# Value products turned round, a sum of exponentials by TensorE, and one accumulator in the last step

## The chip, the cores and the metric

The kernel runs on one core of one Trainium2 chip. The metric is the device time of one execution in microseconds (us). Before the change it is 943.63 us, the median of 3 runs (942.25 to 943.75).

## The reference

```python
def _attn_ref(q, k, v, agents):            # q, k, v: 2 x 12480 x 128, agents: 2 x 49 x 128
    def sm(a, b):
        s = scale * (a @ b.transpose(0, 2, 1))
        s = s - s.max(-1, keepdims=True)
        e = np.exp(s)
        return e / (e.sum(-1, keepdims=True) + 1e-09)
    a2k = sm(agents, k)                    # 49 x 12480 per batch
    agent_v = a2k @ v                      # 49 x 128 per batch
    q2a = sm(q, agents)                    # 12480 x 49 per batch
    return q2a @ agent_v

def _moe_ref(x, w_in, w_out):              # x: 24960 x 128, w_in: 128 x 2048, w_out: 2048 x 128
    h = x @ w_in
    g = np.where(h > 0.0, h, np.exp(np.minimum(h, 0.0)) - 1.0)
    return g @ w_out
```

The weights come as 64-bit floats and are turned into 32-bit ones on the chip. All is computed in 32 bits; the two large products use a high and a low part of each operand.

## The kernel before

Of each batch the 12480 rows are cut into 13 groups of 960, and a group into 8 tiles (R) of 120 rows (TP). The kernel has a prologue, in which batch 0's side of the agents is done and the weights are converted, and then a loop of 416 steps (S) and 4 more (LAG). A step is one half group (480 columns) times 256 of the 2048 hidden columns, so 8 steps (NP) make a half and 16 a group, here called a turn.

What a step does: `p1(s)` multiplies the attention of the half with `w_in` times the agents' values (line 443, six matmuls of 480 columns, with 49 or 50 rows in each half of the array); `elu(s)` takes the exponential on ScalarE (line 449) and the rest of the activation on VectorE (line 451); `split(s)` makes the high part on ScalarE (line 213) and the low part (line 218) on GpSimd in two halves, or, in steps that `is_kept` names, on VectorE in one instruction; `p2(s - 4)` adds the product with `w_out` of four steps earlier (line 479, 12 matmuls of 480 columns, upper and lower 64 rows into the two accumulators `o0` and `o1`). After each half the accumulators are read by VectorE (`ob`, line 491) and ScalarE (`oa`, line 494), added by GpSimd and stored. `is_kept` names two to three of each eight steps; in such a step the activation stays in PSUM, where its tile `h` is held until the low part is made. There are three tiles `h`, used also by the visits below.

The agents' side of batch 1 is spread over the loop in visits: `plan` puts each in a step, and `visit` gets a tile `h` and does two jobs in it. Up to step 75 a visit holds scores of keys (`k`, line 174) and queries (`q`, line 305): 32 matmuls of 49 columns into four strips of 32 rows. In steps 83 to 155 it holds value products (`e`, `ev_pe`, line 233): the exponentials `s_all` of one group, 64 columns of them, are the stationary operand and 129 columns of `v` the moving one (128 values and a column of ones, whose product is the sum of the exponentials). Eight matmuls alternate between the upper and the lower 64 rows of the output. `ev1_out` adds the outcome on VectorE to `sv` (line 248). There are four pairs (`e e`) and five visits of a query job and a value job (`q e`). After the last one `av_pe` (lines 252 and 253) turns `sv` round by a matmul with `dup`, which holds identities, and `av_out` takes the agents' values `av["t"]` and the reciprocal sum `av["rz"]` from PSUM.

In the prologue the same product is done for batch 0 (jobs `v0` to `v12`, accumulated in PSUM), and `o0 o1 o2` are its `ev0_out`, `av_pe` and `av_out`; jobs `f` are matmuls on a tile `warm` whose result nobody uses. The order of the jobs in the prologue is that of the words in the `run(...)` strings, in the loop that of the calls in it (lines 790 to 815), and engines take their instructions in that order. The first `p1` needs `A0` (line 271), which needs `av["t"]` and `av["rz"]`.

In the last step, ScalarE reads `o0` in two halves (line 487), VectorE adds `o1` (line 488), and SyncE issues the two stores.

Of the kernel before, what the change touches and what calls it, by code (L numbers as in the profile page):

```python
# [24 lines left out]
def tile_agent_attention_moe(  # L25
# [201 lines left out]
    ev_ps, av = {}, {}  # L227

    def ev_pe(ps, b, r, rs):
        e = s_all[:, r].rearrange("p t a -> p (t a)")  # L230
        for j in range(R):
            u = ROWS[j % 2]
            nc.tensor.matmul(out=ps[u:u + 64], lhsT=e[:, j * NA:j * NA + 64], rhs=v_t[b, r][:, j, :], start=(r == rs[0] and j < 2), stop=(r == rs[-1] and j >= R - 2))  # L233
        v_t.pop((b, r))

    def ev0_pe(r):
        ev_pe(ev_ps[0], 0, r, range(NR))

    def ev0_out():
        av["sv"] = sm_p.tile([128, VW], F32, tag="sv", name="sv")  # L240
        nc.vector.tensor_copy(out=av["sv"], in_=ev_ps.pop(0))

    def ev1_out(ps, r):
        if r == 0:
            av["sv"] = sm_p.tile([128, VW], F32, tag="sv", name="sv")
            nc.vector.tensor_copy(out=av["sv"], in_=ps)
        else:
            nc.vector.tensor_tensor(out=av["sv"], in0=av["sv"], in1=ps, op=ALU.add)

    def av_pe():  # L250
        ps = attn_bank()
        nc.tensor.matmul(out=ps[:C, 0:NA2], lhsT=av["sv"][:, 0:C], rhs=dup, start=True, stop=True)
        nc.tensor.matmul(out=ps[:NA2, 128:129], lhsT=dup, rhs=av["sv"][:, C:C + 1], start=True, stop=True)
        av["ps"] = ps

    def av_out():
        ps = av.pop("ps")
        attn_free(ps)
        av["t"] = sm_p.tile([C, NA2], F32, tag="avt", name="avt")
        nc.vector.tensor_copy(out=av["t"], in_=ps[:C, 0:NA2])  # L260
        rz = sm_p.tile([NA2, 1], F32, tag="rz", name="rz")
        nc.vector.tensor_scalar(out=rz, in0=ps[:NA2, 128:129], scalar1=1e-9, scalar2=None, op0=ALU.add)
        nc.vector.reciprocal(out=rz, in_=rz)
        av["rz"] = rz

    def A_pe(b, lo, hi, ps=None):
        av[b, lo] = attn_bank() if ps is None else ps
# [156 lines left out]
    def is_kept(s):  # L424
        first = s - s % NP
        steps = visits.values()
        if first + EDGE in steps:
            kind = "late"
        elif first + 1 in steps:
            kind = "early"  # L430
        else:
            kind = "turn" if first // NP % 2 == 0 else None
        return s - first in ((3,7) if s < NP else KEPT[kind])

    def p1(s):
# [31 lines left out]
    def p2(s):  # L467
        j, half, c = at_step(s)
        if c == 0:
            o_t[0] = ps_o.tile([128, 512], F32, tag="o0", name="o0")  # L470
            o_t[1] = ps_o.tile([128, 512], F32, tag="o1", name="o1")
        first, last = c == 0, c == NP - 1
        hi, lo = hi_t.pop(s), lo_t.pop(s)
        jobs = [(w[:, c, i], hi[:, i, :]) for w in (w_lo, w_hi) for i in range(2)]
        jobs += [(w_hi[:, c, i], lo[:, i, :]) for i in range(2)]
        for i, (w, v) in enumerate(jobs):
            for u, r in enumerate(ROWS):
                x = slice(r, r + 64)
                nc.tensor.matmul(out=o_t[u][:, 0:T], lhsT=w[x], rhs=v[x, :], start=first and i == 0, stop=last and i == len(jobs) - 1)  # L479
        if last:  # L480
            oa = o_p.tile([128, T], F32, tag="oa", name="oa")
            ob = o_p.tile([128, T], F32, tag="ob", name="ob")
            pa, pb = o_t[0], o_t[1]
            n = j * G + half * T
            if s == S - 1:
                for x in (slice(0, T // 2), slice(T // 2, T)):
                    nc.scalar.activation(out=oa[:, x], in_=pa[:, x], func=ACTF.Identity, bias=ncs[:, 0:1])
                    nc.vector.tensor_tensor(out=ob[:, x], in0=pb[:, x], in1=oa[:, x], op=ALU.add)
                    nc.sync.dma_start(out=outT[:, n + x.start:n + x.stop], in_=ob[:, x])
                return None  # L490
            nc.vector.tensor_copy(out=ob, in_=pb[:, 0:T])  # L491
# [20 lines left out]
    with tc.manual_schedule():  # L512
        with tc.tile_pool(name="pro", bufs=6) as pro, tc.tile_pool(name="wc", bufs=2) as wc_p:
# [35 lines left out]
            ev_ps[0] = two[:, 0, 0:VW]  # L549

            def busy(n, cols=512):
                for _ in range(n):
# [56 lines left out]
            def w_diag():  # L609
# [17 lines left out]
                "v": ev0_pe,  # L627
# [3 lines left out]
                "o": lambda n: (ev0_out, av_pe, av_out, w_acc, w_diag)[n](),  # L631
# [26 lines left out]
            run("s12 r12 c12 M1 f5")  # L658
            run("M2 M3 f3 M4 M5 Q0 f2")
            run("u0 x0 U2 u1 x1 U4 Q1 Q2 Q3 x2 u3 x3 U6 u5 x4 x5 u7 Q4 Q5 U8 x6 x7 u9 x8 Q6 U10 u11 x9 U12 x10 x11 x12 a5 b5 a6 b6")  # L660
            run("v0 +o3,v9,v10,v11,v12,q1,K0,K1 v1 v2 v3 v4 Q7 f2 v5 Q8 d5 g5 h5 l5 d6 g6 v6 f1 v7 f1 v8 W0 f2 a7 Q9 b7 h6 l6 d7 g7 h7 l7 v9 f2 v10 v11 v12 W1")
            run("o0 o1 W2 o2")
            fill_ps = ps_o.tile([128, 512], F32, tag="o0", name="o0")
            a_banks.update({0: fill_ps, 1: pair[:, 0, :], 2: hk[:, 0, :], 3: fill_ps})
            run("A0 A1 A2 z0 z1 z2")
# [184 lines left out]
```

## Time and profile before

| | before |
|---|---|
| median of 3 runs | 943.63 us |
| profiled execution, its own time | 942.42 us |
| its span, first to last instruction | 940.6 us |
| TensorE, PE (share of the span) | 929.9 us, 99% |
| ScalarE, ACT | 853.1 us, 91% |
| VectorE, DVE | 758.7 us, 81% |
| GpSimd, POOL | 800.7 us, 85% |
| mean granted TensorE clock | 0.999 |

A busy share is an average over the stages, and matmuls are pipelined, so that 99% is not TensorE at its peak. What a change is worth is read from the chain of waits, the work that ended last followed back from the end. A 32-bit matmul stands in the trace as two records, so 32 matmuls of the program are x64 there; products of high and low parts are one record each.

### The profile page before, as it was taken

The page shows a single profiled execution, that of the slowest core. Times are in us where ns is not written, and L with a number is a line of the kernel's source. Part 1 is how long each engine was busy: PE and PEld are TensorE (multiplying, and loading weights), DVE is VectorE, ACT ScalarE, POOL GpSimd, SP SyncE. Part 2 cuts the span into 40 slices and gives each one's busy share as a digit, 9 for nine tenths or more (in the row PEclk, how much of TensorE's full clock was granted, in tenths as well). Part 3 has the DMA queues.
Part 4 walks back from the last instruction along what each step waited for, and adds up shares of the span by engine and source line. Part 5 has one row for each costly group of instructions (what it writes and reads, how often), then busy time and mean ns, then how long its engine had stood idle before and what let it go on. Part 6 is the DMA issues. An engine that isn't in the chain of part 4 may idle for free.

```text
span 940.6 us, 26784 instructions
## 1 busy us (share of the span) xinstructions
PE 929.9 (99%) x11136; PEld 813.8 (87%) x11136; DVE 758.7 (81%) x861; ACT 853.1 (91%) x1024; POOL 800.7 (85%) x686
## 2 busy tenths in 40 slices
PE   8999999999999999999999999999999999999998
PEld 6878889888888888989888888888888888899997
DVE  6877877878878778878878888887888888888876
ACT  4679999999899889999999999999999999999996
POOL 2578898898899899899898898889898898988886
PEclk9999999999999999999999999999999999999999
DMA  9942222242232211012101101011020021001000
GB/s 351 407 160 70 82 97 70 84 116 70 77 100 71 70 43 49 29 44 71 38 22 61 39 28 65 28 46 59 16 81 28 22 71 38 28 13 39 28 22 22
DMA packets 26108, 67.11 MB, mean 71 GB/s; under 512 B 3221, under 2 KB 14955, under 8 KB 25987
## 3 DMA queue, kind: packets, MB, share of 16 engines
q1 hardware_dynamic: 25843, 65.36, 21.1%
q8 instruction: 87, 1.43, 0.6%
q14 instruction: 34, 0.28, 0.1%
q10 hardware_dynamic: 144, 0.05, 0.0%
HBM read 43.11 MB, written 12.78 MB: 59 GB/s over the span
## 4 chain that ended last, share of the span: by engine, by line
PE 95%; DMA 2%; POOL 1%; ACT 1%; issue 0%; DVE 0%; SPq 0%; DVEq 0%; ACTq 0%
PE o L479 57%; PE h L443 29%; PE h L233 3%; PE h L305 2%; PE h L174 1%; DMA raw<-in_w_out_dram 1%; POOL lo L218 1%; DMA k<-in_kT_dram 1%; PE h L553 1%; PE h L343 1%; DMA py<-px 0%; PE h L271 0%; PE o L174 0%; PE o L505 0%; ACT hi L213 0%
## 5 line engine op out<-in xcount | busy, mean ns | idle before, releaser
L218 POOL TENSOR_TENSOR lo<-g,hi 128x480 fp32r<-128x480 f32 x576 | 692.1, 1236 | 45.7 <-ACT hi L213 26.3
L449 ACT ACTIVATE e<-h 128x960 f32<-128x960 f32 x416 | 406.3, 977 | 39.6 <-PE h L443 23.7
L451 DVE SCALAR_TENSOR_TENSOR g<-e,h 128x960 f32<-128x960 f32 x288 | 331.8, 1152 | 117.1 <-ACT e L449 80.3
L213 ACT ACTIVATE hi<-g 128x960 fp32r<-128x960 f32 x288 | 289.4, 1005 | 1.2 <-DVE g L451 1.2
L479 PE MATMUL o<-lo,w_hi 64*128 64x480 f32 x1664 | 258.0, 379 | 0.5 <-POOL lo L218 0.2
L479 PE MATMUL o<-hi,w_lo 64*128 64x480 f32 x1664 | 257.3, 379 | 0.1
L479 PE MATMUL o<-hi,w_hi 64*128 64x480 f32 x1664 | 256.5, 378 | 0.0
L443 PE MATMUL h<-py,ahi 50*128 50x480 f32 x832 | 253.4, 384 | 0.4 <-DMA py<-px 0.4
L443 PE MATMUL h<-px,ahi 50*128 50x480 f32 x832 | 253.2, 384 | 0.1
L479 PEld LDWEIGHTS o<-lo,w_hi 64*128 64x128 f32 x1664 | 165.6, 184 | 22.9 <-POOL lo L218 2.5
L479 PEld LDWEIGHTS o<-hi,w_hi 64*128 64x128 f32 x1664 | 165.4, 184 | 18.4
L479 PEld LDWEIGHTS o<-hi,w_lo 64*128 64x128 f32 x1664 | 164.5, 186 | 18.6 <-issue 0.3
L443 PEld LDWEIGHTS h<-px,ahi 50*128 50x128 f32 x832 | 151.9, 186 | 13.7 <-DVE ob L491 1.1
L443 PEld LDWEIGHTS h<-py,ahi 50*128 50x128 f32 x832 | 152.0, 186 | 11.3 <-issue 0.9
L451 DVE SCALAR_TENSOR_TENSOR h<-e,h 128x960 f32<-128x960 f32 x128 | 148.0, 1156 | 15.0 <-ACT e L449 13.9
L218 DVE TENSOR_TENSOR lo<-h,hi 128x960 fp32r<-128x960 f32 x128 | 147.5, 1152 | 12.7 <-ACT hi L213 12.7
L443 PE MATMUL h<-px,alo 49*128 49x480 f32 x416 | 156.6, 377 | 0.0
L443 PE MATMUL h<-py,alo 49*128 49x480 f32 x416 | 156.5, 376 | 0.0
L213 ACT ACTIVATE hi<-h 128x960 fp32r<-128x960 f32 x128 | 124.6, 974 | 0.0
L495 POOL TENSOR_TENSOR ob<-ob,oa 128x480 f32<-128x480 f32 x51 | 63.2, 1239 | 58.6 <-ACT oa L494 25.5
L443 PEld LDWEIGHTS h<-px,alo 49*128 49x128 f32 x416 | 78.0, 188 | 5.6
L443 PEld LDWEIGHTS h<-py,alo 49*128 49x128 f32 x416 | 78.1, 188 | 4.3
(111 smaller groups left out, 529.3 us busy)
## 6 DMA issues: line engine op xcount, KB each, us to landing
k<-in_kT_dram SPq DMA_DIRECT2D x26, 480.0 KB
q<-in_qT_dram SPq DMA_DIRECT2D x26, 480.0 KB
out_dram<-ob SPq DMA_DIRECT2D x51, 240.0 KB
v<-in_vx_dram SPq DMA_DIRECT2D x13, 483.8 KB
v<-in_vx_dram SPq DMA_DIRECT2D x12, 516.0 KB
py<-px SPq DMA_DIRECT2D x50, 93.8 KB
py<-px SPq DMA_DIRECT2D x50, 91.9 KB
raw<-in_w_in_dram SPq DMA_DIRECT2D x4, 512.0 KB
```

The costliest lines, as they stand in the source:

```text
L174: nc.tensor.matmul(out=ps[u:u + w, j * NA:(j + 1) * NA], lhsT=src[:, x:x + w], rhs=ag_sb[:, b, :], start=True, stop=True)
L213: nc.scalar.activation(out=out, in_=x, func=ACTF.Copy)
L218: eng.tensor_tensor(out=out, in0=x, in1=hi.bitcast(F32), op=ALU.subtract)
L233: nc.tensor.matmul(out=ps[u:u + 64], lhsT=e[:, j * NA:j * NA + 64], rhs=v_t[b, r][:, j, :], start=(r == rs[0] and j < 2), stop=(r == rs[-1 ...
L305: nc.tensor.matmul(out=ps[u:u + w, t * NA:(t + 1) * NA], lhsT=src[:, x:x + w], rhs=ag_sb[:, j // NG, :], start=True, stop=True)
L343: nc.tensor.transpose(ps[:NA2, u, i * HP:(i + 1) * HP], pp[x, i, 0:NA2], ident[x, x])
L443: nc.tensor.matmul(out=h[:, u, 0:T], lhsT=a[x, :], rhs=p[u ^ half][x, :], start=i == 0, stop=i == 2)
L449: nc.scalar.activation(out=e, in_=h, func=ACTF.Exp, bias=-1.0, scale=1.0)
L451: nc.vector.scalar_tensor_tensor(out=g, in0=e, scalar=1.0, in1=h, op0=ALU.min, op1=ALU.max)
L479: nc.tensor.matmul(out=o_t[u][:, 0:T], lhsT=w[x], rhs=v[x, :], start=first and i == 0, stop=last and i == len(jobs) - 1)
L495: nc.gpsimd.tensor_tensor(out=ob, in0=ob, in1=oa, op=ALU.add)
L553: nc.tensor.matmul(out=two[:, 1, 0:cols], lhsT=warm[:, 0:128], rhs=warm[:, 0:cols], start=True, stop=True)
```

## The change

1. `ev_pe` becomes `evt_pe`: `v` is now the stationary operand, in four strips of 32 of its columns, and 49 exponentials the moving one. A group takes 32 matmuls of 49 columns instead of 8 of 129, and the outcome is the agents' values already turned round. `av_pe` and `av_out` go.
2. The sum of the exponentials no longer comes with the product. In batch 0 TensorE sums them with a stationary tile of ones (`Z0` to `Z12`, 4 matmuls of 98 columns each), VectorE folds that (`Y0`) and one matmul adds the partitions (`Y1`). In batch 1 VectorE sums each group's exponentials (`z_red`, from SBUF) and folds them in `z_dup`; one matmul in the visit `A` at step 163 adds the partitions, and `z_out` takes the reciprocal there.
3. In steps 80 to 159 the second half of a turn keeps steps 1, 5 and 7 in PSUM; before, 1 and 7. Subtractions (`e_sub`) and exponentials (`e_exp`) of batch 1 move by one step in places.
4. In the last step all 128 rows go at once into `o1` (6 matmuls instead of 12); `o0` ends a step earlier and is read by ScalarE meanwhile, and the second half of the last store is issued by ScalarE.

```diff
-    def ev_pe(ps, b, r, rs):
-        e = s_all[:, r].rearrange("p t a -> p (t a)")
+    def evt_pe(ps, b, r, rs):
         for j in range(R):
-            u = ROWS[j % 2]
-            nc.tensor.matmul(out=ps[u:u + 64], lhsT=e[:, j * NA:j * NA + 64], rhs=v_t[b, r][:, j, :], start=(r == rs[0] and j < 2), stop=(r == rs[-1] and j >= R - 2))
+            for u in range(0, C, 32):
+                nc.tensor.matmul(out=ps[u:u + 32, 0:NA], lhsT=v_t[b, r][:, j, u:u + 32], rhs=s_all[:, r, j, :], start=r == rs[0] and j == 0, stop=r == rs[-1] and j == R - 1)
...
+    def z_red(r):
+        nc.vector.tensor_reduce(out=m_all[:, :, r], in_=s_all[:, r, 0:R, :].rearrange("p t a -> p a t"), axis=AX.X, op=ALU.add)
+
+    def z_dup():
+        nc.vector.tensor_reduce(out=dup[:TP, 0:NA], in_=m_all, axis=AX.X, op=ALU.add)
+        nc.vector.tensor_copy(out=dup[:TP, ROWS[1]:ROWS[1] + NA], in_=dup[:TP, 0:NA])
...
+        if 80 <= s < 160 and first // NP % 2 == 1:
+            return s - first in (1,5,7)
...
+            if s == S - 1:
+                nc.tensor.matmul(out=o_t[1][:, 0:T], lhsT=w, rhs=v, start=False, stop=i == len(jobs) - 1)
+                continue
...
+        if s == S - 2:
+            o_t[2] = o_p.tile([128, T], F32, tag="oa", name="oa")
+            return lambda: nc.scalar.activation(out=o_t[2], in_=o_t[0][:, 0:T], func=ACTF.Identity, bias=ncs[:, 0:1])
...
-                for x in (slice(0, T // 2), slice(T // 2, T)):
-                    nc.scalar.activation(out=oa[:, x], in_=pa[:, x], func=ACTF.Identity, bias=ncs[:, 0:1])
-                    nc.vector.tensor_tensor(out=ob[:, x], in0=pb[:, x], in1=oa[:, x], op=ALU.add)
-                    nc.sync.dma_start(out=outT[:, n + x.start:n + x.stop], in_=ob[:, x])
+                for x, eng in ((slice(0, T // 2), nc.sync), (slice(T // 2, T), nc.scalar)):
+                    nc.vector.tensor_tensor(out=ob[:, x], in0=pb[:, x], in1=o_t[2][:, x], op=ALU.add)
+                    eng.dma_start(out=outT[:, n + x.start:n + x.stop], in_=ob[:, x])
...
+            def z0_pe(r):
+                if r == 0:
+                    zt.append(ps_o.tile([128, 512], F32, tag="o0", name="o0"))
+                for i in range(4):
+                    nc.tensor.matmul(out=zt[0][32 * i:32 * i + 32, 0:2 * NA], lhsT=ones2[:, 0:32], rhs=s_all[:, r, 2 * i:2 * i + 2, :].rearrange("p t a -> p (t a)"), start=r == 0, stop=r == NR - 1)
...
-            run("v0 +o3,v9,v10,v11,v12,q1,K0,K1 v1 v2 v3 v4 Q7 f2 v5 Q8 d5 g5 h5 l5 d6 g6 v6 f1 v7 f1 v8 W0 f2 a7 Q9 b7 h6 l6 d7 g7 h7 l7 v9 f2 v10 v11 v12 W1")
-            run("o0 o1 W2 o2")
+            run("v0 +o3,v9,v10,v11,v12,q1,K0,K1 Z0 v1 Z1 v2 Z2 v3 Z3 v4 Z4 Z5 Q7 f2 v5 Q8 d5 g5 h5 l5 d6 g6 Z6 v6 Z7 f1 v7 Z8 f1 v8 W0 Z9 Z10 f1 a7 Q9 b7 h6 l6 d7 g7 h7 l7 v9 Z11 Z12 f2 Y0 v10 f1 v11 v12 Y1")
+            run("W1 o0 W2")
...
+            at(-1 + s0 if r == NR - 1 else s0 + (4, 3, -1)[r % 3], z_red, r)
         s0 = visits["e", NR - 1]
-        at(s0 + 2, av_pe)
-        at(s0 + 2, av_out)
+        at(s0 + 2, z_dup)
+        at(s0 + 1, avt_dup)
...
+            if lo == 0:
+                nc.tensor.matmul(out=tile[:NA2, 0, 256:257], lhsT=dup[:TP, :], rhs=onec[:TP, :], start=True, stop=True)
             for i in range(2):
                 A_pe(1, lo + 512 * i, lo + 512 * i + 512, tile[:, i, :])
+            if lo == 0:
+                z_out(tile[:NA2, 0, 256:257])
```

Three places in the order. First TensorE in the prologue, from job `v5` to the end of `v12`; before:

```order
L233 MATMUL h<-v,s_all 64x129 x16
L553 MATMUL h<-warm 128x128
L233 MATMUL h<-v,s_all 64x129 x8
L553 MATMUL h<-warm 128x128
L233 MATMUL h<-v,s_all 64x129 x8
L505 MATMUL o_708<-w_hi,allone 128x512
L505 MATMUL o_708<-w_lo,allone 128x512
L553 MATMUL h<-warm 128x128 x2
L233 MATMUL h<-v,s_all 64x129 x8
L553 MATMUL h<-warm 128x128 x2
L233 MATMUL h<-v,s_all 64x129 x24
```

The same place after, from the end of `v7`'s part on (line 235 is `evt_pe`, line 605 `z0_pe`, line 555 the matmuls nobody uses):

```order
L555 MATMUL h<-warm 128x128
L235 MATMUL h<-s_all,v 32x49 x32
L508 MATMUL o_963<-w_hi,allone 128x512
L508 MATMUL o_963<-w_lo,allone 128x512
L605 MATMUL o_624<-s_all,ones_83 32x98 x8
L555 MATMUL h<-warm 128x128
L235 MATMUL h<-s_all,v 32x49 x32
L605 MATMUL o_624<-s_all,ones_83 32x98 x8
L555 MATMUL h<-warm 128x128 x2
L235 MATMUL h<-s_all,v 32x49 x32
L555 MATMUL h<-warm 128x128
L235 MATMUL h<-s_all,v 32x49 x64
```

The products of the groups now stand in more and shorter runs with the sums between them, and the unused matmuls are as many, but in more places.

Second VectorE at a visit with a query job and a value job (step 107, tiles `mx` and `qe` are the query's, `lo` the low part of a kept step); before:

```order
L491 COPY ob<-o_4600 128x480
L222 TENSOR_TENSOR s_all<-s_all,mb 120x392
L451 SCALAR_TENSOR_TENSOR g<-e,h 128x960
L310 TENSOR_REDUCE mx<-h 124x8
L318 TENSOR_TENSOR qe_87<-h,mx 124x8x49
L248 TENSOR_TENSOR sv<-sv,h 128x129
L451 SCALAR_TENSOR_TENSOR g<-e,h 128x960 x2
L326 TENSOR_REDUCE z<-qe_87 124x8
L222 TENSOR_TENSOR s_all<-s_all,mb 120x392
L451 SCALAR_TENSOR_TENSOR g<-e,h 128x960
L330 RECIPROCAL qz<-z 124x8
```

After:

```order
L247 TENSOR_REDUCE m_all<-s_all 120x49
L494 COPY ob<-o_5090 128x480
L225 TENSOR_TENSOR s_all<-s_all,mb 120x392
L449 SCALAR_TENSOR_TENSOR g<-e,h 128x960
L306 TENSOR_REDUCE mx<-h 124x8
L314 TENSOR_TENSOR qe_90<-h,mx 124x8x49
L244 TENSOR_TENSOR avt<-avt,h 128x49
L449 SCALAR_TENSOR_TENSOR g<-e,h 128x960
L225 TENSOR_TENSOR s_all<-s_all,mb 120x392
L449 SCALAR_TENSOR_TENSOR h<-e,h 128x2x480
L322 TENSOR_REDUCE z<-qe_90 124x8
L449 SCALAR_TENSOR_TENSOR g<-e,h 128x960
```

A sum (line 247) is new ahead of the copy `ob`, the second subtraction stands a step earlier, and one more activation goes to `h`, whose low part follows on VectorE.

Third TensorE at the end of the program; before, the last four of the 12 matmuls:

```order
L479 MATMUL o_14721<-lo,w_hi 128x480
L479 MATMUL o_14722<-lo,w_hi 128x480
L479 MATMUL o_14721<-lo,w_hi 128x480
L479 MATMUL o_14722<-lo,w_hi 128x480
L846 UNCONDITIONAL_BRANCH
```

After, all six of the last step:

```order
L476 MATMUL o_15405<-hi,w_lo 128x480 x2
L476 MATMUL o_15405<-hi,w_hi 128x480 x2
L476 MATMUL o_15405<-lo,w_hi 128x480 x2
L878 UNCONDITIONAL_BRANCH
```

The last step writes one accumulator alone.

## Rows read from the trace of the kernel before

**Rows 1.** The page: shares of the chain that ended last, and the granted clock.
```profile
PEclk9999999999999999999999999999999999999999
PE 95%; DMA 2%; POOL 1%; ACT 1%; issue 0%; DVE 0%; SPq 0%; DVEq 0%; ACTq 0%
```

**Rows 2.** Chain of waits, visits with scores alone: start us, us, what.
```profile
113.56 0.83 PE h L305 x64
114.39 0.69 PE h L174 x64
...
131.05 1.52 PE h L174 x96
```

**Rows 3.** Chain of waits, a visit `e e` and the value part of a `q e`.
```profile
236.87 1.92 PE h L233 x32
...
255.89 1.03 PE h L233 x16
```

**Rows 4.** Chain of waits, the turning round of batch 1's values.
```profile
402.89 0.41 PE h L252 x2
403.30 0.11 PE h L253 x2
```

**Rows 5.** Chain of waits in the prologue.
```profile
34.08 4.56 PE h L233 x80
...
39.63 0.64 PE h L553 x4
40.27 1.91 PE h L233 x32
42.19 0.42 PE h L553 x2
42.61 1.03 PE h L233 x16
...
47.87 2.80 PE h L233 x48
...
51.33 0.21 PE h L252 x2
51.54 0.10 PE h L253 x2
```

**Rows 6.** Chain of waits at the end.
```profile
933.90 2.66 PE o L479 x24
936.57 0.46 ACT oa L487
...
937.05 0.76 DVE ob L488 x2
```

**Rows 7.** Timeline at the end, SyncE's queue: start us, us, instruction.
```profile
937.49 0.81 SPq L489 DMA_DIRECT2D out_dram<-ob  x2
```

**Rows 8.** Groups by form: names, shapes, count | busy us, mean ns | idle before.
```profile
L218 POOL TENSOR_TENSOR lo<-g,hi 128x480 fp32r<-128x480 f32 x576 | 692.1, 1236 | 45.7 <-ACT hi L213 26.3 <-POOL ob L495 10.5 <-POOL lo L218 7.5
L218 DVE TENSOR_TENSOR lo<-h,hi 128x960 fp32r<-128x960 f32 x128 | 147.5, 1152 | 12.7 <-ACT hi L213 12.7
L326 DVE TENSOR_REDUCE z<-qe 124x8 f32<-124x400 f32 x26 | 14.6, 563 | 0.0
L248 DVE TENSOR_TENSOR sv<-sv,h 128x129 f32<-128x129 f32 x12 | 3.4, 283 | 0.1
```

**Rows 9.** Busy time by stretch: us, PE, PEld, DVE, ACT, POOL busy, clock, DMA.
```profile
201.60:236.90 35.30, 35.30 (x493) 29.98 (x494) 29.64 (x37) 33.10 (x40) 31.80 (x27) 1.00 0.30 82
236.90:272.90 36.00, 36.00 (x410) 30.60 (x412) 28.39 (x34) 32.33 (x39) 32.39 (x28) 1.00 0.30 81
254.00:266.00 12.00, 12.00 (x174) 10.07 (x172) 10.62 (x15) 10.22 (x13) 10.52 (x9) 1.00 0.38 104
```

**Rows 10.** Timeline at the visit `A` of step 163, VectorE and ScalarE.
```profile
416.06 1.15 DVE L451 SCALAR_TENSOR_TENSOR g<-e,h 128x960 f32<-128x960 f32 x1
...
416.91 1.02 ACT L281 ACTIVATE ahi<-h,unit,rz 114x256 fp32r<-114x256 f32 x2
```

More of the change, by code (lines that the diff above doesn't have):

```diff
@@ L70, in tile_agent_attention_moe @@
     ones = const.tile([NA, TP], F32)
+    ones2 = const.tile([TP, 32], F32)
+    part = const.tile([128, 1], F32)
+    onec = const.tile([128, 1], F32)
     pp = const.tile([TQ, R // 2, 128], F32)
@@ L225, in e_exp @@
         nc.scalar.activation(out=s_all[:, r, 0:R, :], in_=s_all[:, r, 0:R, :], func=ACTF.Exp, scale=scale)
-    ev_ps, av = {}, {}
-    def ev_pe(ps, b, r, rs):
-        e = s_all[:, r].rearrange("p t a -> p (t a)")
+    av = {}
+    def evt_pe(ps, b, r, rs):
         for j in range(R):
-            u = ROWS[j % 2]
-            nc.tensor.matmul(out=ps[u:u + 64], lhsT=e[:, j * NA:j * NA + 64], rhs=v_t[b, r][:, j, :], start=(r == rs[0] and j < 2), stop=(r == rs[-1] and j >= R - 2))
+            for u in range(0, C, 32):
+                nc.tensor.matmul(out=ps[u:u + 32, 0:NA], lhsT=v_t[b, r][:, j, u:u + 32], rhs=s_all[:, r, j, :], start=r == rs[0] and j == 0, stop=r == rs[-1] and j == R - 1)
@@ L234, in ev_pe @@
         v_t.pop((b, r))
[L236 to L241, printed above, removed]
     def ev1_out(ps, r):
         if r == 0:
-            av["sv"] = sm_p.tile([128, VW], F32, tag="sv", name="sv")
-            nc.vector.tensor_copy(out=av["sv"], in_=ps)
-        else:
-            nc.vector.tensor_tensor(out=av["sv"], in0=av["sv"], in1=ps, op=ALU.add)
@@ L250, in av_pe @@
[L250 to L260, printed above, removed]
+            av["t"] = sm_p.tile([C, NA2], F32, tag="avt", name="avt")
@@ new lines, in ev1_out @@
+            nc.vector.memset(av["t"][:, NA:], 0.0)
+            nc.vector.tensor_copy(out=av["t"][:, 0:NA], in_=ps)
+        else:
+            nc.vector.tensor_tensor(out=av["t"][:, 0:NA], in0=av["t"][:, 0:NA], in1=ps, op=ALU.add)
+    def z_red(r):
[3 more added lines that the diff above has]
+        nc.vector.tensor_copy(out=dup[:TP, ROWS[1]:ROWS[1] + NA], in_=dup[:TP, 0:NA])
@@ L261, in av_out, with z_out, avt_dup @@
+    def z_out(x):
         rz = sm_p.tile([NA2, 1], F32, tag="rz", name="rz")
-        nc.vector.tensor_scalar(out=rz, in0=ps[:NA2, 128:129], scalar1=1e-9, scalar2=None, op0=ALU.add)
+        nc.vector.tensor_scalar(out=rz, in0=x, scalar1=1e-9, scalar2=None, op0=ALU.add)
         nc.vector.reciprocal(out=rz, in_=rz)
         av["rz"] = rz
+    def avt_dup():
+        nc.vector.tensor_copy(out=av["t"][:, ROWS[1]:ROWS[1] + NA], in_=av["t"][:, 0:NA])
     def A_pe(b, lo, hi, ps=None):
@@ L476, in p2 @@
         for i, (w, v) in enumerate(jobs):
+            if s == S - 1:
+                nc.tensor.matmul(out=o_t[1][:, 0:T], lhsT=w, rhs=v, start=False, stop=i == len(jobs) - 1)
+                continue
             for u, r in enumerate(ROWS):
                 x = slice(r, r + 64)
-                nc.tensor.matmul(out=o_t[u][:, 0:T], lhsT=w[x], rhs=v[x, :], start=first and i == 0, stop=last and i == len(jobs) - 1)
+                nc.tensor.matmul(out=o_t[u][:, 0:T], lhsT=w[x], rhs=v[x, :], start=first and i == 0, stop=(last or s == S - 2 and u == 0) and i == len(jobs) - 1)
+        if s == S - 2:
+            o_t[2] = o_p.tile([128, T], F32, tag="oa", name="oa")
+            return lambda: nc.scalar.activation(out=o_t[2], in_=o_t[0][:, 0:T], func=ACTF.Identity, bias=ncs[:, 0:1])
         if last:
-            oa = o_p.tile([128, T], F32, tag="oa", name="oa")
             ob = o_p.tile([128, T], F32, tag="ob", name="ob")
@@ L485, in p2 @@
             if s == S - 1:
-                for x in (slice(0, T // 2), slice(T // 2, T)):
-                    nc.scalar.activation(out=oa[:, x], in_=pa[:, x], func=ACTF.Identity, bias=ncs[:, 0:1])
-                    nc.vector.tensor_tensor(out=ob[:, x], in0=pb[:, x], in1=oa[:, x], op=ALU.add)
-                    nc.sync.dma_start(out=outT[:, n + x.start:n + x.stop], in_=ob[:, x])
+                for x, eng in ((slice(0, T // 2), nc.sync), (slice(T // 2, T), nc.scalar)):
+                    nc.vector.tensor_tensor(out=ob[:, x], in0=pb[:, x], in1=o_t[2][:, x], op=ALU.add)
+                    eng.dma_start(out=outT[:, n + x.start:n + x.stop], in_=ob[:, x])
                 return None
+            oa = o_p.tile([128, T], F32, tag="oa", name="oa")
             nc.vector.tensor_copy(out=ob, in_=pb[:, 0:T])
@@ L548, in tile_agent_attention_moe @@
             two, pair, hk = slot(), slot(), slot()
-            ev_ps[0] = two[:, 0, 0:VW]
             def busy(n, cols=512):
@@ L557, in tile_agent_attention_moe @@
             dve.memset(ones, 1.0)
+            dve.memset(ones2, 1.0)
+            dve.memset(part, 0.03125)
+            dve.memset(onec, 1.0)
             dve.memset(s_all[:, :, R:R + 1, :], 0.0)
@@ L567, in tile_agent_attention_moe @@
             dve.tensor_tensor(out=unit, in0=ident[:, ROWS[0] + NA:ROWS[0] + NK], in1=ident[:, ROWS[1] + NA:ROWS[1] + NK], op=ALU.add)
-            for r in ROWS:
-                for x in ROWS:
-                    dve.tensor_copy(out=dup[r:r + NA, x:x + NA], in_=ident[r:r + NA, r:r + NA])
             idle[:] = [pair[:, i, :] for i in range(2)]
@@ L595, in tile_agent_attention_moe, with z0_out, z0_rz, avt0_out @@
             mb_sb = []
+            zt = []
+            def z0_pe(r):
[3 more added lines that the diff above has]
+                    nc.tensor.matmul(out=zt[0][32 * i:32 * i + 32, 0:2 * NA], lhsT=ones2[:, 0:32], rhs=s_all[:, r, 2 * i:2 * i + 2, :].rearrange("p t a -> p (t a)"), start=r == 0, stop=r == NR - 1)
+            def z0_out():
+                x = zt[0][:, 0:2 * NA].rearrange("p (t a) -> p a t", a=NA)
+                for r in ROWS:
+                    dve.tensor_reduce(out=dup[:, r:r + NA], in_=x, axis=AX.X, op=ALU.add)
+                av["t"] = sm_p.tile([C, NA2], F32, tag="avt", name="avt")
+                dve.memset(av["t"], 0.0)
+            def z0_rz():
+                nc.tensor.matmul(out=zt[0][:NA2, 128:129], lhsT=dup, rhs=part, start=True, stop=True)
+                z_out(zt[0][:NA2, 128:129])
+            def avt0_out():
+                dve.tensor_copy(out=av["t"][:, 0:NA], in_=two[:, 0, 0:NA])
+                dve.tensor_copy(out=av["t"][:, ROWS[1]:ROWS[1] + NA], in_=two[:, 0, 0:NA])
             sums = {}
@@ L626, in tile_agent_attention_moe @@
                 "x": e_exp,
-                "v": ev0_pe,
+                "v": lambda r: evt_pe(two[:, 0, :], 0, r, range(NR)),
+                "Z": z0_pe,
+                "Y": lambda n: (z0_out, z0_rz)[n](),
                 "W": w_sum,
@@ L630, in tile_agent_attention_moe @@
                 "z": lambda c: A_out(0, 512 * c, 512 * c + 512, act),
-                "o": lambda n: (ev0_out, av_pe, av_out, w_acc, w_diag)[n](),
+                "o": lambda n: (avt0_out, None, None, w_acc, w_diag)[n](),
                 "f": lambda n: busy(n, 128),
@@ L690, in visit @@
                 else:
-                    ev_pe(ps[:, 0:VW], 1, n, (n,))
+                    evt_pe(ps, 1, n, (n,))
             if last_max:
@@ L703, in visit @@
                 else:
-                    ev1_out(ps[:, 0:VW], n)
+                    ev1_out(ps[:, 0:NA], n)
         def plan(s, what):
@@ L756, in tile_agent_attention_moe @@
             else:
-                at(x + 7 if r % 3 == 2 else x + 2, e_sub, r)
-            at(s0 - (4 if r % 3 == 0 else 3), e_exp, r)
+                at(x + 7 if r % 3 == 2 else x + 1, e_sub, r)
+            at(s0 - (5 if r % 3 == 0 else 3), e_exp, r)
             at(visits["e", r - 5] + 1 if r > 4 else NM * 4 + 2 * r, load_v, 1, r)
+            at(-1 + s0 if r == NR - 1 else s0 + (4, 3, -1)[r % 3], z_red, r)
         s0 = visits["e", NR - 1]
-        at(s0 + 2, av_pe)
-        at(s0 + 2, av_out)
+        at(s0 + 2, z_dup)
+        at(s0 + 1, avt_dup)
         def A_visit(lo):
             tile = slot()
+            if lo == 0:
+                nc.tensor.matmul(out=tile[:NA2, 0, 256:257], lhsT=dup[:TP, :], rhs=onec[:TP, :], start=True, stop=True)
             for i in range(2):
                 A_pe(1, lo + 512 * i, lo + 512 * i + 512, tile[:, i, :])
+            if lo == 0:
+                z_out(tile[:NA2, 0, 256:257])
             parts = []
```

## The prediction

> **What bounds the kernel now.** [...] The reader is to see two things: the changed products have the very form of the scores, which the trace of before prices, and a turn with scores takes 35.3 us where one with values takes 36.0, TensorE busy throughout in both.
>
> **Part by part.** Own time of the profiled execution 942.42 (span 940.6 and 1.82 around it); it is 1.21 below the median of the runs, so I add the sum to the median.
>
> *Value products of batch 1.* A group becomes 32 matmuls of 49 columns in four strips, as a score job is (there with 128 rows in the array, here with 120). Two score jobs take 1.52, one after a query job 0.69 [rows 2]; two value jobs take 1.92, one after a query job 1.03 [rows 3]. Four pairs save 4 x 0.40 = 1.60, five single ones 5 x 0.34 = 1.70: -3.30. The stretches say the same: 36.0 - 35.3 = 0.7 a turn against 0.40 + 0.34. New is only that the eight tiles add into the same 49 columns, where scores go to fresh ones. If that makes every group as dear as the first job of a visit (0.83 [rows 2]), 13 x 0.14 = 1.8 of it are lost; better than the scores it can't be, since the form is the same. I take the scores' price: -3.30, bounds -3.3 and -1.5.
>
> *Turning round and sum of batch 1.* The two matmuls of `av_pe` go, 0.41 + 0.11 [rows 4]; one matmul of one column comes in visit `A`, 0.11 by the second of these. -0.41, bounds -0.52 and -0.2.
>
> *VectorE in the loop.* 13 sums at 0.563, by the nearest row that sums as many elements from SBUF, are 7.3; five more low parts at 1.152 are 5.8; the 13 additions shrink from 129 to 49 columns, at most 0.283 each [rows 8]. GpSimd gives ten half low parts at 1.236 away, 12.4. Over a turn VectorE goes from 28.4 to 28.4 + 3 x 0.56 + 1.15 = 31.2 of some 35.3, against 29.6 in the busiest score turn, in which TensorE didn't wait [rows 9]. But it is not even: in the 12 us around a visit with a query and a value job VectorE is busy 10.62 now [rows 9], gets 0.56 + 1.15 and loses 0.1 or so, which is 12.2 in 11.7. So some 0.5 a turn can't be hidden there and must be caught up later. What is late then is the activation of a step, and behind it the tile `h`: TensorE has three, the kept step holds one longer, and `p1` of a later step waits for it. Two of the three sums of a turn fall in gaps in which VectorE waits for ScalarE; the third stands ahead of the copy `ob` and of an activation. Five such places at 0.5 give 2.7; if the distance of four steps to `p2` and the freer GpSimd take all of it, 0. I take 0.14 a place, nearer to 0 because VectorE is idle for 4 us of the turn: +0.7, bounds 0 and 2.7.
>
> *Visit A at step 163.* ScalarE now needs the reciprocal that VectorE makes behind the step's activation. That ends at 417.2, ScalarE began at 416.9 [rows 10]; with two tiny instructions between it begins some 0.6 later. Its cover is that TensorE then works on parts made four steps earlier: 0, bounds 0 and 0.7 if that cover is gone.
>
> *Prologue.* The chain there is TensorE without a break, its unused matmuls included [rows 5], so what counts is its sum. Value products now: 4.56 + 1.91 + 3 x 1.03 + 2.80 = 12.36 for 13 groups (the 1.03 stands three times). After: 13 x 0.69 = 8.97. The sums `Z` are new to the trace: four matmuls of 98 columns in four strips; eight such fours of 49 columns take 0.69, so twice the columns are 0.17, 13 x 0.17 = 2.24. A run after another form begins 0.83 - 0.69 = 0.14 dearer [rows 2], and the order has eight runs: 1.12. Together 12.33, which is 0.03 less. The unused matmuls stay eight, but a run of two costs 0.64 and of one 0.42 [rows 5], and two runs of two and four of one (2.96) replace three of two and two of one (2.76): +0.2. The turning round goes, 0.21 + 0.10 [rows 5], a one-column matmul comes: -0.21. VectorE's copies lie beside the sums of the weights that TensorE does next. -0.04, bounds -1.4 (runs begin free, and the unused matmuls cost nothing more) and +1.8 (each `Z` at 0.31, as if each began a run).
>
> *The end.* After the last matmul stand ScalarE 0.46 and VectorE 0.76 [rows 6], and the second store is issued behind the first (two in 0.81 from 937.49, so at about 937.9 [rows 7]). After, ScalarE reads `o0` beside the last matmuls, VectorE begins 0.48 earlier, and the second store needn't wait for the first: 0.5 less. Against it TensorE changes form for its last six matmuls. The rate is no worse: 24 now take 2.66 two by two, 0.22 a pair [rows 6], and six whole ones replace six pairs. Beginning with the whole array costs 0.20, as the unused matmuls show: one 0.42, a second 0.22 more [rows 5]. -0.30, bounds -0.5 and 0.
> [...]
>
> Sum: -3.30 - 0.41 + 0.7 + 0 - 0.04 - 0.30 = -3.35. By its own time 942.42 becomes 939.1; from the median 943.63 it is **940.3**.
>
> **The rivals.**
> *VectorE becomes the bound (slower).* Place: steps 91 to 96 and the same steps of the four turns behind. Price: if the sum and the additional low part stand in TensorE's way whole, 5 x (0.56 + 1.15) = 8.6 on the -4.05 of the other terms: +4.5, 948.1. It decides from 4.05 / 5 = 0.81 a place on. For it: the 12.2 in 11.7. Against: VectorE idles 36.0 - 28.4 = 7.6 in a turn [rows 9], and GpSimd, whose low parts free the buffers of the activations, has 12.4 less to do.
> *The gain is partly given back.* The delay per place is near its 0.5, or the prologue is some 1.8 longer: -3.35 + 2 = 942.3. For it: both unknown terms have more room upwards. Against: in a score turn VectorE, ScalarE (33.1) and GpSimd (31.8) were as busy as they will be, apart from VectorE's 1.6 more [rows 9].
> *Many short matmuls are bound by their issue.* Then each of the 26 groups costs 0.83 as a first job does: 13 x 0.14 in the visits and as much in the prologue, +3.6: 943.9. For it: 0.83 / 32 = 26 ns a matmul is a round figure for that. Against: the second job of a visit does 32 in 0.69, 21.6 ns each [rows 2].
> [...] The trace has 0.69 and a record every 11 ns, so it stays a small chance.
> *The turned products are no cheaper than the old ones (slower, the change doesn't do what it says).* Adding eight times into the same columns would have to cost what the fewer columns save: visits 0 instead of -3.30, prologue 2.24 + 0.2 - 0.21 = +2.2: 943.63 + 2.2 - 0.41 - 0.30 + 0.7 = 945.8. Against: each 32-bit matmul is two records that already add into the same columns, and runs at that price in the scores.
>
> **How the numbers follow.** Forecast 0.69, with its own range 938.2 to 941.7 (VectorE 0 and the prologue at its lower bound; VectorE at 2.1); partly given back 0.14; issue 0.05; VectorE the bound 0.08; no cheaper 0.04. About 0.2%, 1.9 us, is what a measurement of this kernel can tell from no change, so faster means below 941.7 and slower above 945.5. Faster: the forecast and a fifth of the second case, 0.72. Same: the rest of the second case and issue, 0.16. Slower: the last two, 0.12. The range leaves out the two slower cases and ends in the second one: 938.0 to 943.4.
>
> **What would show it.** Right: in the chain of waits a pair of value jobs at 1.5 and a single one behind a query job at 0.7; a turn of values at 35.3 to 35.5; no two matmuls of batch 1's turning round; VectorE busy about 31 in such a turn; the first `p1` within a microsecond of its present place; VectorE directly behind the last matmul. Wrong: TensorE idle before line 443's successors with VectorE as the releaser, near steps 94 to 97 of a turn (VectorE term too small); a value job of 0.8 or more (issue, or adding into the same columns); `Z` pieces of over 0.25 (prologue).

## The result and the profile after

The changed kernel takes 955.66 us (median of 4 runs, 955.27 to 955.74) against 943.39 (4 runs): a ratio of 1.0129, interval 1.0114 to 1.0145. It is slower by 1.3%; a faster kernel was forecast, 940.3, and the measured time lies outside the range of 938.0 to 943.4. The profiled execution has a span of 953.9 us, 13.3 more than before. In the shares of the chain of waits "issue", time in which an engine waits for nothing that the profile shows, has risen from 0% to 2% [rows 1]:

```profile
PE 95%; issue 2%; DMA 1%; ACT 1%; POOL 1%; DVE 1%; SPq 0%; DVEq 0%; ACTq 0%
```

The place is the prologue. Its stretch of the chain of waits after (start us, us, what), to be held against [rows 5]:

```profile
33.42 0.84 PE h L235 x64
...
34.43 0.42 PE h L235 x35
34.85 3.43 issue
38.28 0.51 PE h L235 x27
...
40.63 4.21 issue
...
48.18 2.76 issue
...
54.27 1.47 PE h L235 x64
...
71.74 0.85 PE h L441 x6
```

The first `p1` stands at 71.74, before it stood at 53.65: 18.1 us later. Between `v0` and `p1` TensorE waits six times for "issue", 12.5 us in all. The rest is TensorE's own rows: 25.8 us of them stand between `v0` and `p1` where before there were 19.6, mostly because a row takes longer at the lower clock, as the 1.47 of `v5` (granted clock 0.50) beside the 0.84 of `v0` (1.00). (`v0` begins 0.7 earlier than before.) The gaps don't stand at the beginning of a job, where a wait for a tile would be: `v1` stops after 35 of its 64 records and goes on after 3.43 us. The profile shows no engine and no tile that it waited for.

The busy time by stretch (us, busy PE, PEld, DVE, ACT, POOL, then clock, DMA share, GB/s) shows the same, after:

```profile
40.00:50.00 10.00, 3.96 (x152) 3.42 (x144) 3.67 (x6) 1.50 (x3) 2.23 (x2) 0.50 1.03 403
50.00:60.00 10.00, 8.48 (x292) 7.07 (x296) 3.47 (x4) 3.61 (x8) 5.40 (x7) 0.68 0.38 150
```

and before, in the first of them:

```profile
40.00:50.00 10.00, 10.00 (x137) 8.62 (x137) 7.64 (x11) 6.06 (x12) 8.08 (x9) 1.00 1.03 407
```

The granted clock is 1.00 from 34 to 39, 0.50 from 40 to 55, behind the first long gap, and 1.00 again from 60 to 65. (It was low for most of 8 to 15 as well, 0.54; that cost nothing, `v0` begins at 33.42 against 34.08 before.) The loads fill the DMA engines up to 53 in both kernels: a share of 1.03 before and 1.00 after from 50 to 53, 0.40 and 0.39 from 53 to 55. Among the DMA queues one, q8, carries instructions (packets, MB, share of 16 engines). On the page of before, with TensorE's records beside it, and on that of after:

```profile
PE 929.9 (99%) x11136; PEld 813.8 (87%) x11136; DVE 758.7 (81%) x861; ACT 853.1 (91%) x1024; POOL 800.7 (85%) x686
q8 instruction: 87, 1.43, 0.6%
...
q8 instruction: 98, 1.61, 0.7%
```

A packet has 16.4 KB (1.43 MB by 87). The queue is TensorE's: 87 packets of 256 instructions would be 22272, and 11136 matmul records with as many weight loads are 22272; after, 98 packets hold 25088, and 24956 are counted. The start of each packet, to half a microsecond:

| kernel | packets of queue q8 begin at (us) |
|---|---|
| before | 24.0, 30.0, 36.5, 44.0, 52.5, 58.0 |
| after | 22.5, 29.5, 35.5, 42.0, 48.5, 53.0, 56.5, 60.0, 64.0, 68.0 |

Each long gap ends some 2 to 3 us after a packet begins: 35.5 and 38.28, 42.0 and 44.85, 48.5 and 50.94. While the loads run, packets come 6 to 6.5 us apart from 29.5 on.

The loop did what was forecast. Visits after (chain of waits) [rows 2, 3]:

```profile
254.64 1.55 PE h L235 x122
...
272.43 0.83 PE h L301 x64
273.26 0.71 PE h L235 x64
```

VectorE by stretch, a turn of values and the 12 us around a query and a value job [rows 9]:

```profile
254.60:289.90 35.30, 35.30 (x558) 30.29 (x560) 31.25 (x39) 32.34 (x40) 30.47 (x26) 1.00 0.30 83
271.00:283.00 12.00, 12.00 (x226) 10.35 (x224) 11.89 (x17) 10.77 (x15) 9.88 (x9) 1.00 0.36 105
```

In the view of waits (us in total, times, longest) TensorE has one new wait from the loop's start to 950, near 421.7; the two others, 0.4 and 0.2, are there before as well:

```profile
PE h L441 <- DVE g L449: 0.4, 1, 0.4
```

From the query visit at step 75 to the double one at step 171 before needs 212.76 us (219.82 to 432.58), after 209.67: -3.09.

The end, by the timeline (start, us, instruction) [rows 6, 7]:

```profile
949.80 0.60 PE L476 MATMUL o<-lo,w_hi 128*128 128x480 f32 x2
950.49 0.72 DVE L490 TENSOR_TENSOR ob<-o,oa 128x240 f32<-128x240 f32 x2 [3.43 <-ACT oa L483]
```

VectorE begins directly behind the last matmul (it ends at 950.40).

### The profile page after: what moved, and what is told of

The parts are those of the page before. It is cut to its first block, busy times and chain, and to the rows that moved or that the text cites. A ratio compares the mean times of both kernels' runs of the same rounds, so it can differ in the third digit from the quotient of the medians.

```text
span 953.9 us, 29468 instructions
## 1 busy us (share of the span) xinstructions
PE 932.2 (98%) x12478; PEld 803.0 (84%) x12478; DVE 770.8 (81%) x884; ACT 851.1 (89%) x1023; POOL 786.9 (82%) x676
## 4 chain that ended last, share of the span: by engine, by line
PE 95%; issue 2%; DMA 1%; ACT 1%; POOL 1%; DVE 1%; SPq 0%; DVEq 0%; ACTq 0%
PE o L480 56%; PE h L441 29%; PE h L235 2%; PE h L301 2%; PE h L177 2%; PE h L555 1%; PE o L177 1%; POOL lo L221 1%; PE h L339 1%; DMA k<-in_kT_dram 1%; ACT e L447 0%; PE o L605 0%; PE h L267 0%; DMA py<-px 0%; ACT hi L216 0%
## 5 line engine op out<-in xcount | busy, mean ns | idle before, releaser
L221 POOL TENSOR_TENSOR lo<-g,hi 128x480 fp32r<-128x480 f32 x566 | 678.9, 1235 | 50.7 <-ACT hi L216 25.5
L449 DVE SCALAR_TENSOR_TENSOR g<-e,h 128x960 f32<-128x960 f32 x283 | 326.0, 1152 | 101.4 <-ACT e L447 73.4
L480 PE MATMUL o<-lo,w_hi 64*128 64x480 f32 x1660 | 251.0, 377 | 0.4 <-POOL lo L221 0.2
L480 PE MATMUL o<-hi,w_hi 64*128 64x480 f32 x1660 | 250.7, 377 | 0.0
L480 PEld LDWEIGHTS o<-lo,w_hi 64*128 64x128 f32 x1660 | 159.0, 184 | 25.4 <-POOL lo L221 2.3
L480 PEld LDWEIGHTS o<-hi,w_hi 64*128 64x128 f32 x1660 | 158.6, 184 | 22.8
L480 PEld LDWEIGHTS o<-hi,w_lo 64*128 64x128 f32 x1660 | 158.1, 186 | 20.5
L449 DVE SCALAR_TENSOR_TENSOR h<-e,h 128x960 f32<-128x960 f32 x133 | 153.8, 1156 | 15.1 <-ACT e L447 14.0
L221 DVE TENSOR_TENSOR lo<-h,hi 128x960 fp32r<-128x960 f32 x133 | 153.3, 1152 | 12.6 <-ACT hi L216 12.5
L216 ACT ACTIVATE hi<-h 128x960 fp32r<-128x960 f32 x133 | 129.6, 974 | 0.4 <-DVE h L449 0.3
```

The source lines that it names most:

```text
L216: nc.scalar.activation(out=out, in_=x, func=ACTF.Copy)
L221: eng.tensor_tensor(out=out, in0=x, in1=hi.bitcast(F32), op=ALU.subtract)
L449: nc.vector.scalar_tensor_tensor(out=g, in0=e, scalar=1.0, in1=h, op0=ALU.min, op1=ALU.max)
```

## The experiments

Theory **supply**: TensorE's instructions are fetched by DMA in packets, and the changed prologue runs through them faster than they come. A group with its sum is 36 matmuls, 72 records each of which has a weight load: 144 instructions for some 1.0 us of work. Before it was 32 for 1.03. Rivals: the turned products wait for operands of their own; their form is slow; the loop does something to the start. Ratios are to runs of the kernel before that were taken beside each experiment (medians 943.05 for 1 to 4, 943.12 for 5 and 6, 943.50 for 7).

**1. Batch 0 as before, all else as changed.**

```diff
-                "v": lambda r: evt_pe(two[:, 0, :], 0, r, range(NR)),
+                "v": ev0_pe,
-                "o": lambda n: (avt0_out, None, None, w_acc, w_diag)[n](),
+                "o": lambda n: (ev0_out, av_pe, av_out, w_acc, w_diag)[n](),
-            run("W1 o0 W2")
+            run("o0 o1 W2 o2")
```

> Batch 0's value products, their turning round and the order of the prologue as in the kernel before; batch 1's products turned, its sums on VectorE, the kept steps and the last step's products as in the changed kernel. Theory 'supply' (the changed prologue lost its time because TensorE's instructions, which come in packets of 16 KB, 256 instructions each, came 6.0 to 6.5 us apart there): first p1 within 1 us of 53.7 as before, no gap of over 1 us put down to 'issue' in the runs of the value products, and the time is the kernel before's less what loop and end gained in the changed trace (0.33 at the end, 3 to 4.4 in the loop): 939 to 940.3, a ratio of 0.996. Rival 'elsewhere' (the loss comes from something that the changed loop does to the start, as the loads' order or a buffer): part of the 18 us stays, over 945.

Measured: 939.53 us (5 runs, 938.80 to 940.06), 0.9961 of before, interval 0.9948 to 0.9975. The first `p1` in its chain:

```profile
53.69 0.85 PE h L469 x5
```

It is back at its place, and the runs of the value products have no gap. The whole loss sits in batch 0's part of the change, and this version is faster than both kernels.

**2. Before, with as many instructions a group as after.**

```diff
     def ev0_pe(r):
         ev_pe(ev_ps[0], 0, r, range(NR))
+        for i in range(28):
+            x = 32 * (i % 4)
+            nc.tensor.matmul(out=extra[0][x:x + 32, 0:NA], lhsT=extra[1][:, x:x + 32], rhs=extra[1][:, 0:NA], start=True, stop=True)
```

> The kernel before with 28 more matmuls of 49 columns in four strips behind each of batch 0's 13 groups (364 in all, on a tile of zeros, into an unused bank): as many instructions a group as in the changed prologue, but the value products as before. Theory 'supply': long 'issue' gaps of 2 to 5 us in the prologue, packets of instructions still 6 to 6.5 us apart while the loads run, the clock at its lower level behind the gaps, first p1 at 70 to 76, time 960 to 966. Rival 'operands' (the turned products wait for something of their own, as their weights from tiles that land late): no gaps, only the added work of 13 x 28 x 22 to 26 ns, 8 to 9.5 us: first p1 at 62 to 63, 951 to 953.

Measured: 963.13 us (ratio 1.0213, 1.0194 to 1.0231). Its chain (line 240 is the added work):

```profile
37.30 1.95 issue
...
42.89 2.66 issue
...
49.52 0.20 PE h L346 x2
49.72 1.92 issue
...
74.62 0.85 PE h L446 x6
```

The gaps come without any turned product, and one of them (49.72) stops a transposition that the change doesn't touch. Packets begin at 36.5, 43.0, 49.0, then 52.5, 57.0, 61.0. The rival of the operands falls, since gaps come without them, and so does that of the form: the added matmuls cost 0.74 a group, 9.6 in all, and the time rose by 20.

**3. Fewer bytes to load.**

```diff
-        cuts = (0, R // 2, R) if b == 0 and r == NR - 1 else (0, R)
+        cuts = (0, 1) if b == 0 else (0, R)
...
-lhsT=v_t[b, r][:, j, u:u + 32]
+lhsT=v_t[b, r][:, j if b else 0, u:u + 32]
```

> The changed kernel, but of each of batch 0's 13 value tiles only an eighth is loaded, and all eight products of a group read that eighth (left out: seven eighths of batch 0's values). 5.9 MB of loads less, at 405 GB/s 14.5 us, so the loads end near 39 in place of 53.5. Theory 'supply, held up by the loads': from there on packets of instructions come every 3.5 to 4 us as they do in the changed trace after 53, gaps shrink to under 1 us each, the first p1 comes 8 to 12 us earlier (60 to 64), time 943 to 948. Rival 'supply at a fixed rate' (packets 6 us apart whatever else moves): gaps and p1 as in the changed kernel, 71, time 954 to 956.

Measured: 951.64 us (1.0092, 1.0079 to 1.0106), `p1` at 67.74. The time lies between the two theories, and the run didn't do what it was meant to, as its stretches show:

```profile
30.00:35.00 5.00, 4.73 (x155) 4.05 (x154) 3.97 (x11) 2.40 (x6) 3.04 (x5) 1.00 0.36 103
...
40.00:45.00 5.00, 3.10 (x128) 2.88 (x127) 4.09 (x6) 1.47 (x3) 2.25 (x2) 0.70 0.92 305
```

Only 30 to 35 had few loads (103 GB/s, a quarter of what the changed kernel moves there), and there the gap was 0.62 in place of 3.43; from 37 the small pieces filled most of the engines again, and gaps of 3.13 and 4.09 came back.

**4. Half the instructions.**

```diff
+        w = 32 if b else 64
...
-            for u in range(0, C, 32):
+            for u in range(0, C, w):
...
-                for i in range(4):
+                for i in range(2):
```

> The changed kernel with batch 0's products in two strips of 64 columns (16 matmuls a group for 32) and its sums in two (2 for 4): half the instructions, and by the scores of the prologue, which have this form, 1.06 to 1.10 a group in place of 0.83, and Z about 0.25. TensorE's own work of the prologue is then 4 us over the kernel before's. Theory 'supply': 468 instructions more than before in place of 1456, two packets of 256 for six; the gaps come to 0 to 4 us, the first p1 at 57 to 62, time 944 to 949. Rival 'operands' or 'form': the gaps stay as they are, some 13 us, p1 at 72 to 75, time 954 to 959.

Measured: 947.12 us (1.0043, 1.0029 to 1.0057). Its longest gaps:

```profile
37.85 1.05 issue
...
44.13 1.03 issue
...
62.45 0.84 PE h L442 x6
```

Gaps of 2.6 us in all for 12.5, although its products and sums take more of TensorE (1.07 a group). The granted clock was 1.00 from 30 to 60 in this run. The loads ran to 53 here as well; what fell is the number of instructions. (The expectation miscounts it: a group with its sum is 72 instructions, so 936 in all, 520 and not 468 more than before.) That `p1` is at 62.45, just over my 62, is mostly own work: a `Z` takes 0.35, where I had taken 0.25.

**5. Batch 0's values loaded once.**

```diff
     def load_v(b, r, pool=v_p):
+        if b == 0 and r:
+            v_t[b, r] = one_v[0]
+            return
```

> The changed kernel, but of batch 0's 13 value tiles only the first is loaded and all 13 groups read it (left out: twelve of batch 0's thirteen value tiles). Run e3_few_loads was meant to end the loads at 39 and didn't: its small pieces moved at 230 to 300 GB/s and kept the 16 engines 90% busy from 37 to 48. Here 6.2 MB are gone whole, so only some 2 MB (o3, q1, K0, K1) are left behind 34 and the loads end near 40. Theory 'supply, held up by the loads': packets of instructions 6 us or more apart only up to 40, then 3.5 to 4; at most one gap of over 2 us; first p1 at 56 to 63, time 942 to 948. Rival 'fixed rate': packets 6 us apart throughout, first p1 at 70 to 72, time 953 to 956.

Measured: 949.27 us (1.0061, 1.0047 to 1.0075), `p1` at 65.56. The time lies between the two theories. The chain and one stretch:

```profile
35.36 2.47 issue
...
43.41 1.87 issue
...
51.26 1.48 issue
...
65.56 0.86 PE h L447 x6
```

```profile
40.00:45.00 5.00, 2.85 (x171) 2.44 (x160) 4.24 (x6) 2.01 (x4) 2.25 (x2) 0.90 0.02 3
```

The DMA engines idle from 40 on (share 0.02), packets then come at 42.5, 46.0, 50.5, 53.5, 57.5, so 3 to 4.5 us apart, and TensorE still waits. So the loads are a part of the cause and not the whole: with none from 40 on, 6.2 of the 18 us go (71.74 to 65.56), 11.9 stay (65.56 to 53.69, experiment 1). My error in the expectation was to take the 3.5 to 4 us of an unloaded stretch for harmless.

**6. Experiment 1 without the kept steps 1, 5 and 7.**

```diff
-        if 80 <= s < 160 and first // NP % 2 == 1:
-            return s - first in (1,5,7)
```

> Run e1_first_as_before without the kept steps 1, 5 and 7 of five half turns: GpSimd makes those steps' low parts again, as before. If giving GpSimd's ten half low parts to VectorE is worth something (GpSimd frees the buffers earlier), this is 0.5 to 3 us slower than e1's 939.5: 940 to 942.5. If VectorE's extra work was what cost (my +0.7), it is 0 to 1 us faster: 938.5 to 939.5. If neither is on the path: 939.5, no difference.

Measured: 939.73 us (5 runs, 938.96 to 940.31; 0.9960 of before, 0.9946 to 0.9975). Some 1.3 us is what the intervals could tell; no difference from experiment 1 is seen. TensorE's one wait for VectorE, 0.4, is in experiment 1 and not here, so the kept steps have a part in it; it is too small to show in these times.

**7. The supply measured by itself.** Experiment 1 with two trains of small matmuls.

```diff
+            def train(n):
+                for i in range(n):
+                    x = 32 * (i % 4)
+                    nc.tensor.matmul(out=two[x:x + 32, 1, 0:NA], lhsT=warm[:, x:x + 32], rhs=warm[:, 0:NA], start=True, stop=True)
...
+            train(256)
             run("u0 x0 U2 u1 x1 U4 Q1 Q2 Q3 x2 u3 x3 U6 u5 x4 x5 u7 Q4 Q5 U8 x6 x7 u9 x8 Q6 U10 u11 x9 U12 x10 x11 x12 a5 b5 a6 b6")
...
             run("A0 A1 A2 z0 z1 z2")
+            train(256)
```

> Run e1_first_as_before with the disputed supply measured by itself: two trains of 256 matmuls of 49 columns in four strips (zeros by zeros into an unused bank; each train is 1024 instructions, with a weight load and two passes for each), the first behind the first query scores, at about 33, while the loads fill the 16 engines, the second behind the first products of step A, behind the loads' end. Theory 'supply' (runs e3 and e5 showed that packets stand 3.5 to 4.5 us apart even without loads): the first train takes 4 packets at 6 to 6.5 us, less one or two that are there already, 14 to 26 us; the second 4 at 3.5 to 4.5, less the same, 8 to 18 us; gaps put down to 'issue' every 256 instructions; the time 960 to 985. Rival 'form' (the matmuls themselves are slow when nothing else is between): each train is busy without gaps for 256 x 21.6 to 26 ns, 5.5 to 6.7 us, 951 to 954.

Measured: 970.03 us (2 runs; 1.0281, 1.0205 to 1.0357). The chain through both trains:

```profile
38.77 1.59 PE h L589 x127
40.36 2.68 issue
...
46.77 2.84 PE h L589 x128
49.62 0.61 issue
...
70.40 2.31 PE h L589 x200
72.71 1.57 issue
74.28 1.59 PE h L589 x128
75.87 1.86 issue
77.73 1.59 PE h L589 x128
79.33 2.41 issue
```

Between two gaps stand 127 or 128 records, each with its weight load: 256 instructions, and 16.4 KB by 256 is 64 bytes each. Without loads (a DMA share of 0.01 to 0.02 from 70 to 80) TensorE runs them in 1.59 us at a granted clock of 1.00, and from the start of one such block to the start of the next it takes 3.45 to 4.0 us. At a granted clock of 0.50 (46.77) the same 128 take 2.84, the gap shrinks to 0.61, and the sum is again 3.45: where supply decided, the slower clock cost nothing.

The first train takes 17.0 us, the second 12.1, both within what the supply theory gave. But the first is not the test beside the loads that it was meant to be. Its packets begin at 36.0, 40.5, 44.0, 47.5 and 51.5, and the DMA engines' share falls from 1.02 (35 to 40) to 0.22 (40 to 45) and 0.01 (45 to 50). So all but its first gap are those of an unloaded supply; the 6 to 6.5 us beside the loads rest on the packets of the changed kernel and of experiment 2.

## Why the prediction was wrong

*The step that failed* is the prologue: "The chain there is TensorE without a break, its unused matmuls included [rows 5], so what counts is its sum." I costed it at -0.04, bounds -1.4 and +1.8, and it became +18.1. The sum of TensorE's work was nearly right: at a granted clock of 1.00, 0.84 for each of the twelve runs of groups (I had counted eight), 0.7 for `v12` and 0.17 for a `Z`, 13.0 in all for my 12.33. But it ceased to be what counts. Before, the prologue's 13 groups are 416 instructions; after, with the sums, 1872. At 144 instructions in 1.0 us a packet of 256 is used up in under 2 us, and the next one takes 3.5 to 4 us alone and 6 to 6.5 beside the loads. The granted clock of 0.50 behind the gaps added to it (`v5` 1.47 for 0.84). Experiments 2 and 4 show the number of instructions to be the cause, 7 the rate without loads, 5 that the loads from 40 on are a third of it, and 1 that all of the loss lies in batch 0's part.

I had a rival about issue, "many short matmuls are bound by their issue", at +3.6 with a chance of 0.05. It priced the engine's own rate, which is fine (64 matmuls in 1.55 in the loop), and not the delivery of the instructions. No case of mine held the result. The trace of before had the sign, in the scores of its prologue:

```profile
25.22 0.35 PE h L174 x5
25.57 0.97 issue
26.53 0.93 PE h L174 x26
```

A packet of that kernel begins at 24.0, and the gap ends 2.5 us behind it, as the long gaps do. So the scores of the prologue, which run in this form in two strips, seem to have run out of instructions once already; no run tested this gap. I passed over this row.

*The terms of the loop* held, as a sum. Forecast for the stretch of the values -3.30 - 0.41 + 0.7 = -3.01; measured -3.09. A pair takes 1.55 (forecast 1.52), a single one 0.71 (0.69). VectorE is busy 31.25 in a turn (forecast 31.2) and 11.89 in the 12 us around a visit (12.2 in 11.7). What was off: a sum over a group's exponentials takes 0.87, not 0.56, as the groups by form show [rows 8]:

```profile
L247 DVE TENSOR_REDUCE m_all<-s_all 120x49 f32<-120x392 f32 x13 | 11.4, 874 | 0.0
```

That the 31.25 came out is luck. Three sums of a turn cost 0.9 more than forecast, and the three subtractions of the turn, for which I had no term, 1.0 less (the turn of [rows 9] before, then the one after):

```profile
L222 DVE TENSOR_TENSOR s_all<-s_all,mb 120x392 f32<-120x392 f32 x3 | 2.8, 946 | 0.0
...
L225 DVE TENSOR_TENSOR s_all<-s_all,mb 120x392 f32<-120x392 f32 x3 | 1.8, 609 | 0.0
```

The wait is near my +0.7 by luck as well. I had 0.14 at each of five visits; at four of them TensorE didn't wait at all. Its one wait, 0.4, comes behind the last value visit, right after `z_dup`, a fold and a copy of 1.6 us that my VectorE term left out:

```profile
418.96 0.81 DVE L250 TENSOR_REDUCE dup<-m_all 120x49 f32<-120x637 f32 x1
419.81 0.80 DVE L251 COPY dup<-dup 120x49 f32<-120x49 f32 x1
420.52 1.14 DVE L449 SCALAR_TENSOR_TENSOR g<-e,h 128x960 f32<-128x960 f32 x1
...
421.72 0.48 PE L441 MATMUL h<-px,ahi 50*128 50x480 f32 x1 [0.36 <-DVE g L449]
```

The kept steps have a part in it too, since without them the wait is gone (experiment 6). Pairs and singles save 4 x 0.37 + 5 x 0.32 = 3.1, a little less than my 3.30. The turning round saves 0.23 for my 0.41: its one-column matmul takes 0.29 in visit `A`, not 0.11. With the 0.4 of the wait that is -2.9; the measured -3.09 has 0.1 more, which stays open. So the sum came out nearer than its terms.

From the first `p1` to the end the profiled execution gained 4.8. Some 1.4 of that belong to no term. A third of it is spread over turns in which nothing is changed (499.14 to 825.86 before, 513.73 to 840.00 after: 0.45 less, 0.14%), which is as far as the runs of one kernel lie apart; the rest I leave open.

*Visit A*: ScalarE begins at 432.01, behind the reciprocal, and no wait of TensorE follows; 0 as forecast [rows 10]. The two matmuls of [rows 4] are gone, as forecast.

*The end*: from the last matmul to the span's end 3.5 us for 4.1, against it 0.34 in which TensorE's weight loads stand idle ahead of the six whole matmuls. From the last four records of the step ahead (934.61 before, 948.28 after) to the span's end it is 0.3 less; forecast were 0.30.

With the prologue left alone the other terms give -3.30 - 0.41 + 0.7 - 0.30 = -3.3. Experiment 1 measured 939.53 against 943.05, 3.5 less; so at those places less on TensorE's chain was about as much less of the whole.

## What to carry to other kernels

Cutting one matmul into many small ones costs instructions as well as columns, here 144 a group in place of 32: count the instructions per microsecond of the stretch (a record and its weight load are two) and hold them against what these runs got, 256 per 3.5 to 4 us, or per 6 to 6.5 us where loads filled the DMA engines. This loop paid nothing for a short burst: a turn of values has 558 records, 1116 instructions, in 35.3 us, and in the view of waits no matmul of its visits, 256 instructions in 1.55 us, waits for "issue". And "issue" gaps in the middle of a run, without a releaser, are to be held against the instruction queue of the DMA view before a change adds instructions there.

## What the hardware showed that was not expected

Instructions came more slowly beside the loads: 6 to 6.5 us from one packet to the next at a DMA share of 1.03, 3 to 4.5 at 0.02. How the loads hold a packet up is not shown. TensorE went on some 2 to 3 us after a packet's transfer began (2.4 to 2.9 at the three long gaps of the changed kernel). And the turned form with 49 columns adds eight tiles into the same columns at almost no price: a pair of such groups takes 1.55, a pair of scores 1.52 [rows 2].
